# Window attention and a two-layer network in float32: weight-sum stores spread over a walk, two small tiles moved, and other start times for some DVE and ACT steps

## The chip, the cores and the metric

One Trainium2 chip, of which one core runs the kernel. The metric is the time of one execution on the device in microseconds (us); less is better.

## The reference

Sliding-window attention (8 batches, 8 heads, 576 positions, head size 64, window 64) feeds a network with a leaky activation:

```python
scores = scale * np.matmul(q, k.transpose(0, 1, 3, 2))
mask = (rel >= 0) & (rel < window)                     # rel = query position - key position, window 64
scores = np.where(mask, scores, -1000000000.0)
scores = scores - np.max(scores, axis=-1, keepdims=True)
attn = np.exp(scores)
attn = attn / (np.sum(attn, axis=-1, keepdims=True) + 1e-09)
attn_out = np.matmul(attn, v)
x = np.ascontiguousarray(attn_out.transpose(0, 2, 1, 3)).reshape(B * S, H * D)   # 4608 x 512
h = x @ w_in                                           # 512 x 2048
g = np.maximum(0.01 * h, h)
out = g @ w_out                                        # 2048 x 512
```

Everything is float32.

## The kernel before, in words

**Products.** A float32 product is made of three matmuls on a high and a low part of each operand (high x high, high x low, low x high). So every operand of the network exists twice, and a "high" step (ACT, a copy that rounds) is followed by a "low" step (DVE, what the rounding left).

**Stages.** The 4608 tokens are nine chunks of 512; the attention works on pairs of units (64 query positions of one batch each), `m` = 0 to 35. PE goes through these stages:

1. An order written out by hand (0 to about 130 us): attention of the first pairs, the first chunk, and the conversion of all weights into high and low parts (`bits`, `sign`, `abs`, `clamp`, `join`, `chi`, `rest`).
2. A walk of 32 steps `n` (about 129 to 352 us). A step has a first product (12 matmuls, line 855, in two halves), then on ACT the activation (line 869) and the high part (line 872), on DVE the low part `gs` (line 875, called low(n) below), and two steps later a second product (4 groups of 3, line 864). So the first product of step n + 2 stands on PE behind low(n).
3. For six chunks, seven products instead of eight on halves of the operands (`m`, line 1006), their sums on DVE (line 1015), the activation and the split, and the second product (`y`, line 1031), in three phases up to the end. `x_build` (lines 790 to 835) makes the sums of the attention's results that these products need.

The attention of pairs 8 to 35 is woven into stages 2 and 3. For one pair: S scores (PE, line 266); E scale and mask (DVE, 650); P the largest over partitions (POOL, 659); B subtract (DVE, 666); X exp (ACT, 670); A the sum over partitions (POOL, 662); c brings the sum's row into a tile of 128 x 8 (a DMA on SP, 673; one for each half, 64 partitions each); I adds 1e-9 and inverts (DVE, 677 and 678); rows writes it to HBM (SP, 681); spread reads it back over 64 partitions (SP, 694, twice); V the product with the values (PE, 706); take (ACT, 713); Y multiplies by the inverse (DVE, 717); keep stores the pair's result (SP, 720). From pair 20 on there is no take, and Y reads PSUM. The target of c, `compact0` or `compact1`, is used by every second pair; A of the next pair overwrites the tile `late_o` that c reads, so A waits for that DMA.

**Weight sums.** The seven products need sums of weight blocks. 40 stores on SP's DMA queue (24 of 256 KB to `w_first`, 16 of 512 KB to `w_second`: 14.7 MB) write them from the tiles in which the converted weights stand (`both`, named p or pfew in the profile; line 623). They are read again by POOL's DMAs (line 993) in stage 3.

**What sets the order.** Stages 2 and 3 are ordered by a planner in the kernel (`op`, `load`, `bulk`, `arrange`): each step has an engine, an estimated length, the steps that it follows, a rank, a `lag` (how long after its last predecessor it may start in the plan) and a `land` (how long a DMA's result takes). The planner always takes the earliest possible start, and among the steps that are ready then the lowest rank. Each engine and each DMA queue then executes its list in that order; the numbers themselves wait for nothing on the chip. The stores have rank 2.0, behind nearly everything that is ready, but are ready as soon as the weights are.

**Places in memory.** Tiles of the pool `const` come first in each partition, then the working tiles. Before the change the operands of the network (p, pfew, pxa, pxb) start 64 bytes past a multiple of 128; the tiles `gs0`, `gs1`, `q`, `k` are in `const` and start on multiples of 128.

Of the kernel before, what the change touches and what calls it, by code (L numbers as in the profile page):

```python
# [13 lines left out]
F32 = mybir.dt.float32  # L14
# [3 lines left out]
ALU = mybir.AluOpType  # L18
# [6 lines left out]
P = 128  # L25
# [58 lines left out]
FT = DF // P  # L84
# [13 lines left out]
def band_attention_ffn(ctx: ExitStack, tc: tile.TileContext, qT, kB, vW, vL, w_in, w_out, eye_mask, out, outT):  # L98
    nc = tc.nc
# [18 lines left out]
    half = FT // 2  # L118
# [69 lines left out]
    def first_at(f, k, n=1):  # L188
        return w_first[:, 512 * (7 * f + k) :][:, : 512 * n]
# [205 lines left out]
    def open_room():  # L395

        e, n, f = (wk.tile([P, 512, 2], U32, tag="raw", bufs=3, name=f"late_{x}") for x in "enf")
        e, n, f = (flat(x).bitcast(F32).rearrange("p (a b) -> p a b", a=2) for x in (e, n, f))
        r = flat(wk.tile([P, NP, 2, D], F32, tag="y", bufs=1, name="late_r").rearrange("p a b c -> p a (b c)"))
        o = [wk.tile([P, 512], F32, tag="o", name=f"late_o{i}") for i in range(2)]  # L400
        later.update(e=e, n=n, f=f, r=r, o=o)

    def e_of(m):
        return probs_of if m % 3 == 0 else later["ef"[m % 3 - 1]]
# [106 lines left out]
    def load(fn, *after, rank=1.0, us=0.5, land=4.0):  # L511
        return op("SP", us, fn, *after, rank=rank, land=land)
# [72 lines left out]
        t = pairs_of_g[n % 2] if n % 4 < 2 else own(("g", n // (2 * FT)), F32R)[:, n % 2]  # L585
        return t[:, 0], t[:, 1]

    compact = [const.tile([P, 8], F32, name=f"compact{i}") for i in range(2)]
    rows = dram.tile([NU // 2, 1024], F32, name="rows")
    x_rows = dram.tile([NU // 2, P, 512], F32, name="x_rows")  # L590

# [30 lines left out]
    def store(to, f, *cut):  # L622
        nc.sync.dma_start(to, both[f][cut])

    def store_all():
        for f in range(half):
            for x, a, k in ((f, 0, 0), (f, 256, 4), (f + half, 256, 5)):
                to = first_at(f, k).rearrange("p (i c) -> p i c", i=2)
                fn = partial(store, to, x, slice(None), slice(2), slice(a, a + 256))
                stores[x].append(load(fn, *ready[x], rank=2.0))  # L630
        for f in range(FT):
            to = w_second[f // 2, :, f % 2].rearrange("p (i c) -> p i c", i=2)
            stores[f].append(load(partial(store, to, f, slice(None), slice(2, 4)), *ready[f], rank=2.0))

    store_all()

# [15 lines left out]
    def sum_of(j):  # L652
        return later["o"][j]
# [16 lines left out]
        nc.scalar.activation(e, e, AF.Exp)  # L670

    def compact_of(m, j):
        nc.sync.dma_start(compact[m % 2][64 * j : 64 * j + 64], sum_of(j)[:1].rearrange("a (p b) -> a p b", b=8))

    def inverse_of(m):
        c = compact[m % 2]
        nc.vector.tensor_scalar_add(c, c, 1e-9)
# [82 lines left out]
    def normalise(m):  # L760

        late = 0.0 if early(m) else 0.5
        o, before, two, after = at[m], at.get(m - 1, {}), at.get(m - 2, {}), at.get(min(m + 2, EARLY - 1))
        if "v" in o and before:
            o["v"]["after"].append(before["V"])
        o["I"] = op("DVE", 0.4, partial(inverse_of, m), o["c0"], o["c1"], rank=0.8 + late)
        o["rows"] = load(partial(rows_of, m), o["I"], rank=0.3 + late)
        for j in range(2):
            if m + 2 in at:
                at[m + 2][f"c{j}"]["after"].append(o["rows"])  # L770
        spread = [load(partial(spread_of, m, j), o["rows"], before.get("Y"), rank=0.3 + late) for j in range(2)]
        if early(m):
            free = [after["E1"], before.get("take"), o["I"]]
        else:
            free = [both_free if early(m - 2) else two["Y"]]
        o["V"] = op("PE", 1.0, partial(values_of, m), o.get("v"), o["X0"], o["X1"], *free, before.get("V"), rank=0.5 + late, lag=LAG if early(m) else 2 * LAG)
        kept = two.get("kept", [])
        if early(m):
            o["take"] = op("ACT", ACTS, partial(take_of, m), o["V"], *kept, rank=0.5 + late)
        o["Y"] = op("DVE", TWO if early(m) else ONE, partial(product_of, m), *spread, o.get("take"), o["V"], *kept, rank=0.8 + late)  # L780
        if m < UPC // UNITS * LEAD:
            hi = op("ACT", ACTS, partial(high_early, m), o["Y"], *x2_free, rank=0.8 + late)
            o["kept"] = [op("DVE", TWO, partial(low_early, m), hi, rank=0.8 + late)]
# [6 lines left out]
    def x_build(s, n, xt_at, xt_free, x_free):  # L790

        urge = 1.0 if s else 0.2
        m = (UPC * LEAD + 2 * UPC * s) // UNITS + 2 * n

        def raw():
            return g_tile(xt_at[0])[:, :1024].rearrange("p (i q c) -> p i q c", i=2, q=4)

        def sums():
            return g_tile(xt_at[1])[:, 1024 * (s == 0) :][:, :1024].rearrange("p (k i c) -> p k i c", k=4, i=2)

        def part(q):
            return raw()[:, :, q] if q < 4 else sums()[:, q - 4]

        def fetch(i):
            nc.sync.dma_start(g_tile(xt_at[0])[:, 512 * i : 512 * (i + 1)], x_rows[m + i])

        got = [load(partial(fetch, i), *at[m + i]["kept"], *xt_free, rank=urge) for i in range(2)]

        def sub(to, a, b):
            nc.vector.tensor_tensor(part(to), part(a), part(b), ALU.subtract)  # L810

        d = op("DVE", 0.5, partial(sub, 4, 0, 2), *got, rank=urge)
        d3 = op("DVE", 0.5, partial(sub, 6, 1, 0), *got, rank=urge)
        d2 = op("DVE", 0.5, partial(sub, 5, 1, 4), d, rank=urge)
        d4 = op("DVE", 0.5, partial(sub, 7, 3, 5), d2, rank=urge)

        def x_view(i, a, b):
            t, k = x_all(a)
            t = t.rearrange("p k i (n c) -> p k i n c", n=4)[:, k : k + b - a, i, n]
            return t.rearrange("p k (i c) -> p k i c", i=2)  # L820

        def source(a, b):
            if a < 3:
                return raw()[:, :, 1 + a : 1 + b].rearrange("p i k c -> p k i c")
            return sums()[:, a - 3 : b - 3]

        done = []
        for a, b, after in ((0, 2, got), (2, 3, got), (3, 7, [d, d2, d3, d4])):
            hi = op("ACT", 0.2 + 0.213 * (b - a), lambda a=a, b=b: nc.scalar.copy(x_view(0, a, b), source(a, b)), *after, *x_free, rank=urge)

            def low(a=a, b=b):
                nc.vector.tensor_tensor(x_view(1, a, b), source(a, b), x_view(0, a, b).bitcast(F32), ALU.subtract)
# [72 lines left out]
    for n, (c, f) in enumerate(walk):  # L905
        next_main(6 * MM, partial(early_first, n, 0), lows.get(n - 2), *ready[f], *(x2 if c == 2 else ()))
        first = next_main(6 * MM, partial(early_first, n, 1))
        if n == 0:
            next_main(12 * MM, lambda: mm2(*prev))
            s_free = None  # L910
            for i in range(4):
                s_free = op("ACT", 0.65, lambda: due.pop(0)(), main, s_free, rank=0.1)
            evicted[-1] = [s_free] * 4
            gate = op("SP", 0.02, open_room, *all_in, s_free)
        if n > 1:
            second_step(n - 2)
# [18 lines left out]
    for f in range(half):  # L935
# [22 lines left out]
        hurry = 0.4 + 0.15 * f  # L958
        freed = slot_free[14 + f % 2] if f < 2 else prepared[f - 2]
        got = [bulk(partial(fetch, i), *freed, *all_in, rank=hurry + 0.1) for i in range(2)]  # L960
        d1 = op("DVE", 0.5, partial(join_of, 2, (0, 2), (0, 3), ALU.add), *got, rank=hurry)
        d3 = op("DVE", 0.5, partial(join_of, 1, (0, 0), (0, 2), ALU.subtract), *got, rank=hurry)
        d2 = op("DVE", 0.5, partial(join_of, 0, (1, 2), (0, 0), ALU.subtract), d1, rank=hurry)
        d4 = op("DVE", 0.5, partial(join_of, 3, (0, 1), (1, 0), ALU.subtract), d2, rank=hurry)
        hi = op("ACT", 1.07, high, d1, d2, d3, d4, rank=hurry)
# [212 lines left out]
```

## Time and profile before

| what | value |
|---|---|
| time, median of 3 runs | 905.98 us (905.42 to 908.44) |
| the profiled execution's own time | 907.11 us |
| its span in the profile | 905.3 us |
| PE busy in the span | 879.0 us (97%) |
| DVE, ACT, POOL busy | 540.2, 329.5, 362.6 us |
| moved by DMA | 214.49 MB, mean 237 GB/s |

The profiled execution took 1.8 us more than its span, which lies around the first and the last instruction. PE's idle time and the time in which its granted clock is low are what a reordering can change, since the number of matmuls stays. A timeline row reads: start and length in us, engine (q: its queue, which issues DMAs), line, operation, out<-in, shape, how many; in brackets the idle time ahead of it and what ended that. In a row of the view by windows stand the length of the window, then busy time and count of PE, PE's weight loads, DVE, ACT and POOL, then the granted clock, the DMA share and GB/s.

### The profile page before, as it was taken

What the parts mean: (1) busy time and instruction counts of PE and PEld (TensorE: products, weight loads), DVE (VectorE), ACT (ScalarE), POOL (GpSimd) and SP (SyncE); (2) the same over time, 40 slices, a digit from 0 to 9 for tenths busy, and PEclk for the clock granted to TensorE, in tenths of its full rate; (3) what the DMA queues carried; (4) which work ended last, traced back from release to release, by engine and by line L of the source; (5) the groups of instructions that cost most, each with busy time, mean ns of one, the idle gap of its engine ahead of it and who ended that gap; (6) DMA issues with size and microseconds to landing.
All of it is one profiled execution on the core that took longest, in us unless ns stands there. A gap on an engine that the chain in (4) does not pass through costs nothing.

```text
span 905.3 us, 16930 instructions
## 1 busy us (share of the span) xinstructions
PE 879.0 (97%) x6874; PEld 706.9 (78%) x6874; DVE 540.2 (60%) x843; ACT 329.5 (36%) x560; POOL 362.6 (40%) x222
## 2 busy tenths in 40 slices
PE   8999999789999998999999999999999999999998
PEld 5877888578787776877887887788888888888886
DVE  7999686368566965866576756874336323332321
ACT  4666554133233353423333332332334223332221
POOL 5332003388875700877682576881000000100000
PEclk9999999989999999999999999999999999999999
DMA  9774979753567688887989787878577575555661
GB/s 326 240 253 142 340 222 369 276 165 108 162 211 241 191 299 316 259 272 240 285 266 317 258 288 252 271 245 260 193 245 273 196 240 186 185 191 188 218 222 65
DMA packets 82557, 214.49 MB, mean 237 GB/s; under 512 B 16048, under 2 KB 26416, under 8 KB 70960
## 3 DMA queue, kind: packets, MB, share of 16 engines
q0 software_dynamic: 12960, 94.38, 31.4%
q10 hardware_dynamic: 28400, 60.53, 20.4%
q1 hardware_dynamic: 41120, 58.51, 19.5%
q8 instruction: 54, 0.88, 0.4%
q14 instruction: 23, 0.19, 0.1%
HBM read 168.59 MB, written 44.68 MB: 236 GB/s over the span
## 4 chain that ended last, share of the span: by engine, by line
PE 80%; DMA 9%; DVE 7%; issue 2%; ACT 1%; POOL 1%; ACTq 0%; SPq 0%; DVEq 0%; POOLq 0%
PE y L1031 29%; PE m L1006 24%; PE h L855 6%; PE acc L864 5%; PE h L418 4%; PE acc L454 4%; PE s L266 3%; PE o L706 3%; DMA late_r<-rows 2%; DMA compact<-late_o 1%; DMA rows<-compact 1%; DMA x_rows<-late_n 1%; DVE p L946 1%; DMA raw<-w_in 1%; DVE late_n L717 1%
## 5 line engine op out<-in xcount | busy, mean ns | idle before, releaser
L1006 PE MATMUL m<-pfew,p 128*128 128x512 f32 x720 | 172.2, 393 | 5.1 <-DVE pxa L1015 5.1
L1006 PEld LDWEIGHTS m<-pfew,p 128*128 128x128 f32 x720 | 134.4, 188 | 34.5 <-DVE pxa L1015 6.0
L1031 PE MATMUL y<-gs,p 128*128 128x512 f32 x576 | 139.5, 395 | 0.0
L1031 PE MATMUL y<-pxa,p 128*128 128x512 f32 x576 | 136.5, 391 | 0.0
L1031 PEld LDWEIGHTS y<-gs,p 128*128 128x128 f32 x576 | 107.4, 187 | 26.1
L1031 PEld LDWEIGHTS y<-pxa,p 128*128 128x128 f32 x576 | 107.7, 188 | 23.4
L993 POOL DMA_DIRECT2D p<-w_second x48 | 25.7, 535 | 187.2 <-PE y L1031 142.7
L1018 ACT ACTIVATE p<-p 128x512 f32<-128x512 f32 x63 | 39.7, 631 | 114.2 <-DVE p L1015 112.2
L864 PE MATMUL acc<-p,gs 128*128 128x512 f32 x324 | 80.3, 396 | 0.0
L1006 PE MATMUL m<-pxb,p 128*128 128x512 f32 x288 | 73.3, 399 | 3.5 <-ACT p L887 2.5
L659 POOL PARTITION_ALL_REDUCE g<-late_f x20 | 36.5, 1853 | 98.8 <-DVE late_f L650 98.7
L662 POOL PARTITION_ALL_REDUCE late_o<-late_f x20 | 65.1, 3272 | 24.1 <-ACT late_f L670 14.4
L1015 DVE TENSOR_TENSOR p<-m,pxa 128x512 f32<-128x512 f32 x63 | 43.4, 689 | 50.4 <-PE m L1006 50.1
L1024 DVE TENSOR_TENSOR gs<-p,gs 128x512 fp32r<-128x512 f32 x48 | 37.1, 774 | 56.1 <-ACT gs L1021 56.1
L864 PEld LDWEIGHTS acc<-p,gs 128*128 128x128 f32 x324 | 59.9, 188 | 13.3
L993 POOL DMA_DIRECT2D p<-w_first x42 | 22.8, 543 | 114.5 <-PE m L1006 64.7
L662 POOL PARTITION_ALL_REDUCE late_o<-e x18 | 59.2, 3308 | 20.0 <-DMA compact<-late_o 14.2
L1006 PEld LDWEIGHTS m<-pxb,p 128*128 128x128 f32 x288 | 54.4, 192 | 16.0 <-ACT p L887 2.6
L1015 DVE TENSOR_TENSOR pxa<-m,pxa 128x512 f32<-128x512 f32 x57 | 39.1, 686 | 44.7 <-PE m L1006 43.4
L662 POOL PARTITION_ALL_REDUCE late_o<-late_e x18 | 59.6, 3326 | 12.3 <-ACT late_e L670 6.0
L855 PE MATMUL h<-pxa,p 128*128 128x512 f32 x228 | 57.1, 399 | 2.1 <-DVE gs L875 2.1
L1021 ACT CAST gs<-p 128x512 fp32r<-128x512 f32 x48 | 29.7, 620 | 79.4 <-PE y L1031 79.2
(139 smaller groups left out, 1336.4 us busy)
## 6 DMA issues: line engine op xcount, KB each, us to landing
p<-w_second POOLq DMA_DIRECT2D x48, 1024.0 KB, 5.1
p<-w_first POOLq DMA_DIRECT2D x42, 1024.0 KB, 5.8
v<-vL ACTq DMA_DIRECT2D x27, 512.0 KB, 5.9
raw<-w_out ACTq DMA_DIRECT2D x15, 512.0 KB, 4.2
k<-kB ACTq DMA_DIRECT2D x28, 256.0 KB, 4.0
raw<-w_in ACTq DMA_DIRECT2D x14, 512.0 KB, 3.8
late_r<-rows SPq DMA_DIRECT2D x56, 128.0 KB, 4.4
q<-qT ACTq DMA_DIRECT2D x26, 256.0 KB, 4.7
```

Of the source, the lines that this page charges most:

```text
L418: nc.tensor.matmul(ps, a[:, k, :], b[:, k, part], start=n == 0, stop=n == len(terms) - 1)
L454: nc.tensor.matmul(acc[c, i], a[:, ts], b, start=begin and n == 0, stop=end and n == 2)
L659: nc.gpsimd.partition_all_reduce(most_of(j), e_of(m)[:, j], P, ReduceOp.max)
L662: nc.gpsimd.partition_all_reduce(sum_of(j), e_of(m)[:, j], P, ReduceOp.add)
L855: nc.tensor.matmul(ps, a[:, k, :], b[:, k], start=i == 0, stop=i == len(terms) - 1)
L864: nc.tensor.matmul(acc[c, i], a[:, i * P : (i + 1) * P], b, start=begin and k == 0, stop=n in ends and k == 2)
L993: nc.gpsimd.dma_start(ring[n], of)
L1006: nc.tensor.matmul(tiles[b], w[:, 256 * i + 128 * kt : 256 * i + 128 * kt + 128], x_part(OF_X[k], j, kt), start=begin and c == 0, stop=c = ...
L1015: nc.vector.tensor_tensor(to(), tiles[b], x(), ALU.add)
L1018: nc.scalar.activation(to(), to() if b is None else tiles[b], AF.Prelu, alpha=0.01)
L1024: nc.vector.tensor_tensor(g_pair(q)[1], x(), g_pair(q)[0].bitcast(F32), ALU.subtract)
L1031: nc.tensor.matmul(tiles[i], a, b, start=f == 0 and k == 0, stop=f == FT - 1 and k == 2)
```

## The change

Three things.

1. The 40 stores are no longer planned at once. They stand in a list, in the order in which the walk's third chunk uses the weights (blocks 15, 14, 13, 12, 0, 1, ...), and `PACE` = 2 of them are planned behind the first product of each walk step from step 1 on.
2. The two tiles that c fills move from `const` to the pool of working tiles, where they take places of a tag ("sm") that the first stage used before. `const` becomes 64 bytes shorter, so all working tiles start 64 bytes lower: p, pfew, pxa and pxb now start on a multiple of 128.
3. Planner lags grow: I and Y from 0.12 to 0.3 (3.3 from pair 20 on); in `x_build` two differences and the high parts to 0.2 or 2.6; two sums of line 946 (the preparation of combined weights) to 2.0.

All instructions stay the same, in kind and number; their order changes on all five engines from the walk on.

```diff
+PACE = 2
-    compact = [const.tile([P, 8], F32, name=f"compact{i}") for i in range(2)]
+        c = [wk.tile([P, 32], F32, tag="sm", name=f"late_c{i}")[:, :8] for i in range(2)]
-    def store_all():
-        for f in range(half):
-            for x, a, k in ((f, 0, 0), (f, 256, 4), (f + half, 256, 5)):
-                to = first_at(f, k).rearrange("p (i c) -> p i c", i=2)
-                fn = partial(store, to, x, slice(None), slice(2), slice(a, a + 256))
-                stores[x].append(load(fn, *ready[x], rank=2.0))
-        for f in range(FT):
-            to = w_second[f // 2, :, f % 2].rearrange("p (i c) -> p i c", i=2)
-            stores[f].append(load(partial(store, to, f, slice(None), slice(2, 4)), *ready[f], rank=2.0))
+    stored = []
+    for f in turn_of:
+        near, far = f % half, f // half
+        for a, k in ((0, 0), (256, 4)) if far == 0 else ((256, 5),):
+            to = first_at(near, k).rearrange("p (i c) -> p i c", i=2)
+            stored.append((f, partial(store, to, f, slice(None), slice(2), slice(a, a + 256))))
+        to = w_second[f // 2, :, f % 2].rearrange("p (i c) -> p i c", i=2)
+        stored.append((f, partial(store, to, f, slice(None), slice(2, 4))))
...
+        for f, fn in stored[(n - 1) * PACE : n * PACE] if n else ():
+            stores[f].append(load(fn, first, *ready[f], rank=2.0))
...
-        o["I"] = op("DVE", 0.4, partial(inverse_of, m), o["c0"], o["c1"], rank=0.8 + late)
+        o["I"] = op("DVE", 0.4, partial(inverse_of, m), o["c0"], o["c1"], rank=0.8 + late, lag=0.3 + 6 * late)
...
-        o["Y"] = op("DVE", TWO if early(m) else ONE, partial(product_of, m), *spread, o.get("take"), o["V"], *kept, rank=0.8 + late)
+        o["Y"] = op("DVE", TWO if early(m) else ONE, partial(product_of, m), *spread, o.get("take"), o["V"], *kept, rank=0.8 + late, lag=0.3 + 6 * late)
...
-        d = op("DVE", 0.5, partial(sub, 4, 0, 2), *got, rank=urge)
-        d3 = op("DVE", 0.5, partial(sub, 6, 1, 0), *got, rank=urge)
+        d = op("DVE", 0.5, partial(sub, 4, 0, 2), *got, rank=urge, lag=3 * urge - 0.4)
+        d3 = op("DVE", 0.5, partial(sub, 6, 1, 0), *got, rank=urge, lag=3 * urge - 0.4)
...
-        d1 = op("DVE", 0.5, partial(join_of, 2, (0, 2), (0, 3), ALU.add), *got, rank=hurry)
-        d3 = op("DVE", 0.5, partial(join_of, 1, (0, 0), (0, 2), ALU.subtract), *got, rank=hurry)
+        d1 = op("DVE", 0.5, partial(join_of, 2, (0, 2), (0, 3), ALU.add), *got, rank=hurry, lag=2.0)
+        d3 = op("DVE", 0.5, partial(join_of, 1, (0, 0), (0, 2), ALU.subtract), *got, rank=hurry, lag=2.0)
```

What this does to the order, at three places. On SP's queue at the end of the weight conversion, where the first c of the walk (pair 8, line 673 before, 671 after) stands; ahead of these rows stand, before, 15 stores more. Before:

```order
58 L623 DMA w_second<-p_7_90 128x1024
59 L623 DMA w_second<-p_8_91 128x1024
60 L623 DMA w_second<-p_9_92 128x1024
61 L623 DMA w_second<-p_10_93 128x1024
62 L623 DMA w_second<-p_11_94 128x1024
63 L623 DMA w_second<-p_15_1545 128x1024
64 L623 DMA w_second<-p_16_1620 128x1024
65 L623 DMA w_first<-p_17_1768 128x2x256
66 L623 DMA w_second<-p_17_1768 128x1024
67 L673 DMA compact_1571<-late_o_1806 64x1x8
68 L673 DMA compact_1571<-late_o_1807 64x1x8
69 L673 DMA compact_1572<-late_o_1806 64x1x8
```

And of the change:

```order
41 L624 DMA w_first<-p_17_1736 128x2x256
42 L624 DMA w_second<-p_17_1736 128x1024
43 L624 DMA w_first<-p_11_94 128x2x256
44 L624 DMA w_second<-p_11_94 128x1024
45 L671 DMA late_c_1772<-late_o_1770 64x1x8
46 L624 DMA w_first<-pfew_86 128x2x256 x2
47 L671 DMA late_c_1772<-late_o_1771 64x1x8
48 L624 DMA w_second<-pfew_86 128x1024
49 L624 DMA w_first<-pfew_86 128x2x256
50 L671 DMA late_c_1773<-late_o_1770 64x1x8
51 L679 DMA rows<-late_c_1772 128x8
```

All 40 stores stood ahead of the first c; now eight do, and about two stand between every two of the attention's transfers until the walk's step 20.

On DVE near 400 us, in stage 3's first phase: the sums of the products' banks `m_3_1` to `m_3_3` (line 1015), from which the next products on PE get free banks, with Y of pair 20 (line 717 before, 715 after) and I of pair 21 (677 and 678 before, 675 and 676 after). Before:

```order
441 L717 TENSOR_TENSOR late_n<-o_3827,late_r 128x4x2x64
442 L1015 TENSOR_TENSOR pxa_36_3702<-m_3_1_4030,pxa_36_3702 128x512
443 L677 TENSOR_SCALAR compact_1572<-compact_1572 128x8
444 L678 RECIPROCAL compact_1572<-compact_1572 128x8
445 L1015 TENSOR_TENSOR pxa_36_3702<-m_3_2_4040,pxa_36_3702 128x512
```

And of the change:

```order
446 L675 TENSOR_SCALAR late_c_1773<-late_c_1773 128x8
447 L676 RECIPROCAL late_c_1773<-late_c_1773 128x8
448 L1015 TENSOR_TENSOR pxa_36_3701<-m_3_1_4032,pxa_36_3701 128x512
449 L715 TENSOR_TENSOR late_n<-o_3802,late_r 128x4x2x64
450 L1015 TENSOR_TENSOR pxa_36_3701<-m_3_2_4042,pxa_36_3701 128x512
```

I of pair 21 and the bank's first sum moved ahead of Y of pair 20. In the next group of banks, Y of pair 21 stands between `m_4_1` and `m_4_2` as before.

On DVE near 565 us, at the end of the first phase, Y of pair 29 (line 717 before, 715 after) with the last low part of `x_build` (line 832 before, 830 after), the results' copies (line 1034) and the next phase's first sums (line 1015). Before, where that low part stands 15 rows higher:

```order
585 L1034 COPY p_25_3027<-y_1_0_5067 128x512
586 L677 TENSOR_SCALAR compact_1571<-compact_1571 128x8
587 L678 RECIPROCAL compact_1571<-compact_1571 128x8
588 L1034 COPY p_23_2923<-y_1_2_5077 128x512
589 L666 TENSOR_TENSOR late_f<-late_f,g 128x512
590 L717 TENSOR_TENSOR late_n<-o_5280,late_r 128x4x2x64
591 L1015 TENSOR_TENSOR pxa_38_5562<-m_0_1_5555,pxa_38_5562 128x512
592 L1015 TENSOR_TENSOR pxa_38_5562<-m_0_2_5565,pxa_38_5562 128x512
```

And of the change:

```order
586 L675 TENSOR_SCALAR late_c_1772<-late_c_1772 128x8
587 L676 RECIPROCAL late_c_1772<-late_c_1772 128x8
588 L715 TENSOR_TENSOR late_n<-o_5362,late_r 128x4x2x64
589 L830 TENSOR_TENSOR pfew_3381<-pxa_35_3675,pfew_3381 128x4x256
590 L1034 COPY p_25_3033<-y_1_0_5084 128x512
591 L664 TENSOR_TENSOR late_f<-late_f,g 128x512
592 L1034 COPY p_23_2921<-y_1_2_5099 128x512
593 L664 TENSOR_TENSOR late_f<-late_f,g 128x512
594 L1015 TENSOR_TENSOR pxa_38_5571<-m_0_1_5564,pxa_38_5571 128x512
```

Y of pair 29 is no longer the row ahead of the next phase's first sum; it now stands ahead of the last low part of `x_build` and of both copies.

More of the change, by code (lines that the diff above doesn't have):

```diff
@@ L400, in open_room @@
         o = [wk.tile([P, 512], F32, tag="o", name=f"late_o{i}") for i in range(2)]
-        later.update(e=e, n=n, f=f, r=r, o=o)
+        c = [wk.tile([P, 32], F32, tag="sm", name=f"late_c{i}")[:, :8] for i in range(2)]
+        later.update(e=e, n=n, f=f, r=r, o=o, c=c)
     def e_of(m):
@@ L623, in store @@
         nc.sync.dma_start(to, both[f][cut])
-    def store_all():
-        for f in range(half):
-            for x, a, k in ((f, 0, 0), (f, 256, 4), (f + half, 256, 5)):
-                to = first_at(f, k).rearrange("p (i c) -> p i c", i=2)
-                fn = partial(store, to, x, slice(None), slice(2), slice(a, a + 256))
-                stores[x].append(load(fn, *ready[x], rank=2.0))
-        for f in range(FT):
-            to = w_second[f // 2, :, f % 2].rearrange("p (i c) -> p i c", i=2)
-            stores[f].append(load(partial(store, to, f, slice(None), slice(2, 4)), *ready[f], rank=2.0))
-    store_all()
+    stored = []
[6 more added lines that the diff above has]
+        stored.append((f, partial(store, to, f, slice(None), slice(2, 4))))
     def scores_of(m):
@@ L672, in compact_of @@
     def compact_of(m, j):
-        nc.sync.dma_start(compact[m % 2][64 * j : 64 * j + 64], sum_of(j)[:1].rearrange("a (p b) -> a p b", b=8))
+        nc.sync.dma_start(later["c"][m % 2][64 * j : 64 * j + 64], sum_of(j)[:1].rearrange("a (p b) -> a p b", b=8))
     def inverse_of(m):
-        c = compact[m % 2]
+        c = later["c"][m % 2]
         nc.vector.tensor_scalar_add(c, c, 1e-9)
@@ L680, in rows_of @@
     def rows_of(m):
-        nc.sync.dma_start(rows[m].rearrange("(p b) -> p b", b=8), compact[m % 2])
+        nc.sync.dma_start(rows[m].rearrange("(p b) -> p b", b=8), later["c"][m % 2])
     def done_of(m):
@@ L828, in x_build @@
         for a, b, after in ((0, 2, got), (2, 3, got), (3, 7, [d, d2, d3, d4])):
-            hi = op("ACT", 0.2 + 0.213 * (b - a), lambda a=a, b=b: nc.scalar.copy(x_view(0, a, b), source(a, b)), *after, *x_free, rank=urge)
+            hi = op("ACT", 0.2 + 0.213 * (b - a), lambda a=a, b=b: nc.scalar.copy(x_view(0, a, b), source(a, b)), *after, *x_free, rank=urge, lag=3 * urge - 0.4)
             def low(a=a, b=b):
```

## The prediction

> **What bounds the kernel now.** I read the page first, then the waits, then the windows of the stretches in which PE idles, and last the timeline around each. The page's first part:
>
> ```profile
> PE 879.0 (97%) x6874; PEld 706.9 (78%) x6874; DVE 540.2 (60%) x843; ACT 329.5 (36%) x560; POOL 362.6 (40%) x222
> ```
>
> PE is the bound: of the span of 905.3 us it leaves 905.3 - 879.0 = 26.3 us idle, some 6 of them at the two ends. A reordering can only win idle time and slow-clock time. Who makes PE wait, and what makes those wait:
>
> ```profile
> PE h L855 <- DVE gs L875: 10.0, 2, 7.9
> PE m L1006 <- DVE pxa L1015: 5.1, 3, 2.0
> POOL late_o L662 <- DMA compact<-late_o: 22.0, 6, 14.2
> DVE late_n L717 <- DMA late_r<-rows: 19.3, 7, 4.2
> ```
>
> The first two rows say that PE waits for low parts and sums on DVE; the last two that the attention's chain waits for small DMAs (c and spread). How the DMAs stand, by windows (the last three columns are granted clock, DMA share, GB/s):
>
> ```profile
> 140.00:175.00 35.00, 35.00 (x356) 28.52 (x356) 18.92 (x25) 11.41 (x21) 11.77 (x5) 1.00 1.00 374
> 175.00:190.00 15.00, 7.10 (x84) 5.13 (x83) 9.81 (x9) 3.95 (x7) 13.85 (x6) 0.77 0.31 89
> 190.00:250.00 60.00, 60.00 (x629) 48.16 (x627) 41.07 (x51) 20.55 (x37) 50.44 (x21) 1.00 0.47 142
> 250.00:313.00 63.00, 63.00 (x616) 50.34 (x612) 48.08 (x69) 20.01 (x34) 44.04 (x18) 1.00 0.72 227
> 313.00:321.00 8.00, 5.93 (x46) 4.41 (x46) 6.77 (x9) 5.49 (x10) 2.22 (x1) 0.79 0.26 80
> 353.00:361.00 8.00, 4.47 (x49) 3.38 (x39) 6.71 (x15) 3.86 (x7) 0.00 (x0) 0.79 0.57 184
> 565.00:575.00 10.00, 8.02 (x56) 6.15 (x55) 7.26 (x13) 2.99 (x6) 7.73 (x5) 0.83 0.88 280
> ```
>
> The DMA engines are full up to 175 us, then PE idles and its clock drops (0.77), and afterwards the engines are half empty. The largest stall, gap A, in the timeline:
>
> ```profile
> 147.36 1.46 DVE L239 TENSOR_TENSOR p<-w,p 128x512 fp32r<-128x512 f32 x2
> 153.70 3.23 POOL L662 PARTITION_ALL_REDUCE late_o<-late_f  x1 [0.55 <-ACT late_f L670]
> 156.83 1.86 POOL L659 PARTITION_ALL_REDUCE g<-e  x1
> 158.60 3.31 POOL L662 PARTITION_ALL_REDUCE late_o<-late_f  x1
> 156.30 9.92 SPq L623 DMA_DIRECT2D w_second<-p  x7
> 169.42 10.46 SPq L673 DMA_DIRECT2D compact<-late_o  x3
> 168.56 0.59 ACT L872 CAST gs<-h 128x512 fp32r<-128x512 f32 x1 [3.30 <-PE acc L864]
> 176.22 2.20 DVE L677 TENSOR_SCALAR compact<-compact 128x8 f32<-128x8 f32 x1 [9.14 <-DMA compact<-late_o]
> 182.65 0.68 DVE L875 TENSOR_TENSOR gs<-h,gs 128x512 fp32r<-128x512 f32 x1
> 168.54 2.89 PE L855 MATMUL h<-pxa,p 128*128 128x512 f32 x12
> 172.45 3.02 PE L864 MATMUL acc<-p,gs 128*128 128x512 f32 x12
> 183.38 2.93 PE L855 MATMUL h<-pxb,p 128*128 128x512 f32 x6 [7.90 <-DVE gs L875]
> ```
>
> POOL ends the first sum of pair 8 at 153.70 + 3.23 = 156.93 us, but its c is issued on SP only at 169.42, behind the stores. I of pair 8 waits for it on DVE until 176.22, and low(6), whose high part stood ready at 168.56 + 0.59 = 169.15, is queued behind I and a subtraction until 182.65. PE had run dry at 172.45 + 3.02 = 175.47. Had DVE been free, low(6) would have had 175.47 - 169.15 - 0.68 = 5.6 us of slack. Gap A costs 7.90 us, and behind it six matmuls take 2.93 us where twelve take 2.89, so 2.93 - 2.89/2 = 1.5 us more.
>
> The other stalls (B near 313 us, C near 354, D, E, F at 402, 415 and 567), with what DVE did ahead of B and the Y rows ahead of D, E and F:
>
> ```profile
> 308.24 6.99 POOL L662 PARTITION_ALL_REDUCE late_o<-late_e  x2 [2.60 <-ACT late_e L670]
> 308.83 2.73 DVE L717 TENSOR_TENSOR late_n<-late_n,late_r 128x512 f32<-128x512 f32 x1
> 312.19 2.32 DVE L946 TENSOR_TENSOR p<-p 128x256 f32<-128x256 f32 x1
> 315.16 3.05 PE L855 MATMUL h<-pxa,p 128*128 128x512 f32 x9 [2.07 <-DVE gs L875]
> 356.06 0.47 PE L1006 MATMUL m<-pxb,p 128*128 128x512 f32 x1 [2.51 <-ACT p L887]
> 357.54 2.50 PE L1006 MATMUL m<-pxb,p 128*128 128x512 f32 x5 [1.02 <-DVE pxb L832]
> 399.87 0.69 DVE L717 TENSOR_TENSOR late_n<-o,late_r 128x512 f32<-128x512 f32 x1 [3.80 <-DMA late_r<-rows]
> 402.26 1.66 PE L1006 MATMUL m<-pfew,p 128*128 128x512 f32 x6 [1.36 <-DVE pxa L1015]
> 413.75 0.69 DVE L717 TENSOR_TENSOR late_n<-o,late_r 128x512 f32<-128x512 f32 x1 [3.65 <-DMA late_r<-rows]
> 415.10 1.66 PE L1006 MATMUL m<-pfew,p 128*128 128x512 f32 x6 [1.71 <-DVE pxa L1015]
> 565.59 0.69 DVE L717 TENSOR_TENSOR late_n<-o,late_r 128x512 f32<-128x512 f32 x1 [4.18 <-DMA late_r<-rows]
> 567.73 1.78 PE L1006 MATMUL m<-pfew,p 128*128 128x512 f32 x6 [1.98 <-DVE pxa L1015]
> ```
>
> D, E and F have one pattern: Y stands on DVE ahead of a sum that PE needs, and waits there for its spread. B is another: two DVE operations take 2.73 and 2.32 us while POOL reduces (308.24 to 315.23).
>
> **The stores.** Eight of them now stand ahead of the first c. The last weights are converted at 147.36 + 1.46 = 148.8 us; eight stores are 4 x 256 + 4 x 512 KB = 3.1 MB, at the 374 GB/s of the window 8.4 us, and most are ready earlier. So SP should be free when pair 8's first sum ends at 156.9. From its issue to I, c took 176.22 - 169.42 = 6.8 us with the queue full, which bounds its landing: 163.7 for the first half, and for the second, after 158.60 + 3.31 = 161.9 and some 1 us of stores, 169.7. I ends by 171.9. The subtraction queued behind I needs the next sum and maximum on POOL (163.7 + 3.2 + 1.9 = 168.8), so it ends by about 173.5 and low(6) by 174.2, before 175.47 even at this bound: **gap A goes, -9.4** (7.90 + 1.5). The other end is 0, where a transfer of the chain comes 9 us later than this.
>
> The price: the remaining 11.6 MB go over about 120 us beside the walk, 97 GB/s on top of the 142 of the half-empty window, which fits under 374. On SP each c, rows and spread stands behind up to two stores. A store's issue took 9.92/7 = 1.42 us with the engines full, so a chain of three transfers is late by 0 to 8.5 us; low(n) has 5.6 us of slack as counted above. I take +1.5 for one small new stall (between 0 and rival 3 below), nearer to 0 since the engines are not full there.
>
> **The Y and I rows moved.** At D, I of pair 21 and the first sum go ahead of Y of pair 20; the second sum then follows Y directly, 400.48 instead of about 401.6 (I and a sum, 0.6 + 0.6, no longer between), so D's 1.36 shrinks by about 1.1. E: rows of pair 21 is issued earlier by the same move, up to the 3.8 us that Y of pair 20 waited, and Y of pair 21 waited 3.65; the gap of 1.71 goes wholly or by half. **-2.2** together; ends 0 and -3.1. F: Y of pair 29 moves four rows ahead of the sum that PE needs, and its I ahead of the Y before it. Gap F is 1.98 us and the window's clock of 0.83 loses 0.17 x 10 = 1.7. Of these 3.7 I take **-3.0**; ends 0 (Y as late as now, and its wait falls on the last low part of `x_build` in its place) and -3.7.
>
> The Trainium skill, "TensorE: Matmul & The Clock Gate" (Why this matters for your kernels), asks for no idle gaps of PE above about 3 us, since one window of idle halves the clock. By that rule F, a gap of 1.98 us, would cost no clock and its removal win 1.98 at most, and the sum would be 1.0 us smaller. The window around F has the clock at 0.83, so here the measurement decides.
>
> **What I cost at nothing.** B: Y and the differences of line 946 move against low(n), but POOL's long sums keep their total, so such a meeting goes or comes back elsewhere: 0, with -3.8 (2.07 and, by the window with 0.79, 0.21 x 8 = 1.7 of clock) and as much more as ends. C hangs on pair 19's transfers, whose I and Y keep their neighbours on DVE: 0, ends -5.2 (2.51 + 1.02 + 1.7) and +4.2, the length of Y's longest wait. If the attention's chain runs less far ahead than now, C is where it shows. The DVE steps with longer lags win or lose nothing themselves; what covers them is PE's queue, and without it they cost their length, 0.4 to 0.7 us.
>
> **64 bytes lower.** The one trace of a tile's place is this pair of groups, products of equal shape, with the moving operand on a multiple of 128 bytes (gs) and 64 past one (pxa):
>
> ```profile
> L1031 PE MATMUL y<-gs,p 128*128 128x512 f32 x576 | 139.5, 395 | 0.0
> L1031 PE MATMUL y<-pxa,p 128*128 128x512 f32 x576 | 136.5, 391 | 0.0
> L1006 PE MATMUL m<-pfew,p 128*128 128x512 f32 x720 | 172.2, 393 | 5.1 <-DVE pxa L1015 5.1
> L1006 PE MATMUL m<-pxb,p 128*128 128x512 f32 x288 | 73.3, 399 | 3.5 <-ACT p L887 2.5
> ```
>
> 3.0/576 = 5.2 ns a matmul lie between them. It can be the place, that one operand's place differs from the other's (then gs gains once p lies like it), or something else in gs. I take 0; ends -3.0 (gs becomes like pxa) and rival 2.
>
> The Trainium skill, "DMA: Bandwidth & Descriptors" (How a descriptor splits into AXI transactions), says that a descriptor's transactions begin at 256-byte boundaries. A row of 2 KB that starts 192 past one would be 70 beats of 32 bytes, and 68 after the move: an estimate of 3% where DMA is the limit. No run here shows it so far, and the sum leaves it out.
>
> **The sum**: -9.4 + 1.5 - 2.2 - 3.0 = -13.1 us on the profiled execution's 907.11 (span 905.3 and 1.8 around it), so 894.0; that execution is 1.1 above the median, so **892.9** beside 905.98.
>
> **Rivals.**
> 1. Only gap A goes, and the stalls of the Y pattern come back at other places, since spread's latency stays what it is: 905.98 - 9.4 + 1.5 = 898, up to 903 if more new stalls come. For it: Y waited 19.3 us in seven places, and a moved row brings no spread earlier. Against: of 28 Y rows only three stood where PE had to wait.
> 2. The other side: slower matmuls. If a moving operand on a multiple of 128 bytes is what costs 5.2 ns, the 2,772 matmuls with p, pfew, pxa or pxb moving (1,008 at line 1006 by the rows above, 576 of y, and by the program's count 768 in the walk and 420 in the first chunk) take 14.4 us more: 892.9 + 14.4 = 907.3; with only gap A gone, 912. It decides from 13.1/2,772 = 4.7 ns. For it: the difference is in groups without any wait. Against: one pair of groups, and the same operand takes part in both.
> 3. The stores make low(n) late: 8.5 us on a chain of three, less the slack, is 2.9 us, and with 1.5 of clock 4.4 for each of the pairs 8 to 13: 892.9 + 26 = 919. It decides where a store's issue takes over 5.6/6 = 0.93 us. Against: the DMA share of 0.47 and 0.72 there.
> 4. The change doesn't do what it says: the stores ahead of the first c still hold it to 169, and the time stays at 906. Against: the order and 148.8 above.
> 5. All goes well: B or C shrink too, or gs gains its 3.0: 881 to 889.
>
> **How the numbers follow.** The forecast (889 to 897, its own range) has 0.52, rival 1 0.22, rival 2 0.09, rival 3 0.04, rival 4 0.03, the good case 0.10. About 0.3%, 2.7 us, is what a measurement of this kernel can tell from no change. Faster: 0.52 + 0.22 + 0.10 = 0.84; rival 4 and half of rival 2 within: 0.07; slower: 0.09. The range of 885 to 904 leaves out rivals 2 to 4 and the lower part of the good case, together less than 0.2.
>
> **What would show it.** Right, if the profile after has no wait of PE for `gs` above 3 us near 175, c of pair 8 issued before 160, the clock at 1.00 in that window, and fewer than two gaps among D, E and F. The groups of the last fence tell the place: 391 and 395 ns as now, or moved. Wrong, if a wait for `gs` appears between 190 and 275 (rival 3), if Y still waits 4 us ahead of a sum or ahead of `x_build`'s last low part (rival 1), or if gap C grows.

## The result

| | before | after |
|---|---|---|
| median time | 905.70 us (4 runs, 902.73 to 908.44) | 882.51 us (4 runs, 879.38 to 885.29) |
| profiled execution | 907.11 us, span 905.3 | 879.38 us, span 877.6 |
| PE busy in the span | 879.0 us (97%) | 866.8 us (99%) |

The ratio after/before is 0.9744, 95% interval 0.9697 to 0.9791: 23.2 us less, by the interval between 19 and 27. The prediction said 892.9, range 885 to 904: the direction held, the gain was nearly twice the forecast, and the time lies 2.5 us below the range, in the good case of 881 to 889 that had a chance of 0.10. The profiled execution after is the fastest of its four and the one before 1.4 us above its median, so the profiles are 27.7 us apart, 4.5 more than the medians; what follows accounts for the 27.7 of this pair.

The page after says that PE lost 12.2 us of busy time though no matmul was removed, and 15.5 us of idle time (905.3 - 879.0 = 26.3 before, 877.6 - 866.8 = 10.8 now):

```profile
PE 866.8 (99%) x6874; PEld 702.3 (80%) x6874; DVE 548.5 (63%) x843; ACT 329.7 (38%) x560; POOL 364.1 (41%) x222
```

Of the waits (engine, line, what for; us in total, times, longest) these stand against the four of the prediction:

```profile
DVE late_n L715 <- DMA late_r<-rows: 4.4, 4, 2.1
POOL late_o L660 <- DMA late_c<-late_o: 1.2, 2, 0.7
PE m L1006 <- DVE p L1015: 1.2, 1, 1.2
PE h L853 <- DVE gs L873: 0.9, 1, 0.9
PE m L1006 <- DVE pxa L1015: 0.2, 1, 0.2
```

PE's wait for low(n) fell from 10.0 to 0.9 us, for the sums from 5.1 to 1.4; POOL's wait for c from 22.0 to 1.2; Y's wait for spread from 19.3 to 4.4. In the timeline after, the first c of pair 8 and what hung on it:

```profile
152.10 3.23 POOL L660 PARTITION_ALL_REDUCE late_o<-late_f  x1 [0.56 <-ACT late_f L668]
155.36 0.54 SPq L671 DMA_DIRECT2D late_c<-late_o  x1
165.35 0.37 DVE L675 TENSOR_SCALAR late_c<-late_c 128x8 f32<-128x8 f32 x1
173.65 0.59 ACT L870 CAST gs<-h 128x512 fp32r<-128x512 f32 x1 [1.00 <-PE acc L862]
174.27 0.69 DVE L873 TENSOR_TENSOR gs<-h,gs 128x512 fp32r<-128x512 f32 x1 [2.28 <-ACT gs L870]
```

c is issued 0.03 us after POOL's sum ends (152.10 + 3.23 = 155.33), I runs at 165.35 instead of 176.22, and DVE stands waiting for the high part where a low part had been waiting for DVE. All of PE's idle times from 130 us to the end:

```profile
301.66 1.67 PE L853 MATMUL h<-pxa,p 128*128 128x512 f32 x6 [0.87 <-DVE gs L873]
338.60 0.47 PE L1006 MATMUL m<-pxb,p 128*128 128x512 f32 x1 [0.29 <-issue]
339.49 1.42 PE L1006 MATMUL m<-pxb,p 128*128 128x512 f32 x5 [0.42 <-DVE pxb L830]
341.56 7.18 PE L1006 MATMUL m<-pfew,p 128*128 128x512 f32 x29 [0.41 <-DVE pfew L830]
349.90 3.00 PE L1006 MATMUL m<-pxb,p 128*128 128x512 f32 x12 [1.16 <-DVE p L1015]
535.85 1.60 PE L1006 MATMUL m<-pxb,p 128*128 128x512 f32 x6 [0.38 <-issue]
567.38 1.66 PE L1006 MATMUL m<-pfew,p 128*128 128x512 f32 x6 [0.19 <-DVE pxa L1015]
```

Of A (7.90), B (2.07), C (2.51 + 1.02), D, E (1.36, 1.71) and F (1.98), 18.55 us in all, 3.72 are left. No gap is above 1.2 us, and the granted clock is 1.00 in the windows around each: the row of 175 to 190 us, 0.77 before, is

```profile
175.00:190.00 15.00, 15.00 (x210) 12.21 (x210) 8.23 (x11) 4.46 (x8) 10.95 (x5) 1.00 0.80 257
```

The rest is in the matmuls themselves. The groups of lines 1031 and 1006 (busy us, mean ns):

```profile
L1031 PE MATMUL y<-gs,p 128*128 128x512 f32 x576 | 135.4, 390 | 0.0
L1031 PE MATMUL y<-pxa,p 128*128 128x512 f32 x576 | 136.8, 391 | 0.0
L1006 PE MATMUL m<-pfew,p 128*128 128x512 f32 x720 | 171.3, 392 | 0.6 <-DVE pfew L830 0.4 <-DVE pxa L1015 0.2
```

The products with gs moving fell from 395 to 390 ns, 4.1 us in all; those with pxa and pfew moving, which changed their place together with the weights in p, stayed within 1 us.

### The profile page after: what moved, and what is told of

Same layout as the page of the kernel before. It is cut to its first block, busy times and chain, and to the rows that moved or that the text cites. A ratio compares the mean times of both kernels' runs of the same rounds, so it can differ in the third digit from the quotient of the medians.

```text
span 877.6 us, 16928 instructions
## 1 busy us (share of the span) xinstructions
PE 866.8 (99%) x6874; PEld 702.3 (80%) x6874; DVE 548.5 (63%) x843; ACT 329.7 (38%) x560; POOL 364.1 (41%) x222
## 4 chain that ended last, share of the span: by engine, by line
PE 82%; DMA 7%; DVE 6%; issue 2%; ACT 1%; SPq 1%; ACTq 0%; POOL 0%; DVEq 0%; POOLq 0%
PE y L1031 30%; PE m L1006 25%; PE h L420 5%; PE acc L456 5%; PE h L853 5%; PE acc L862 4%; PE s L267 3%; PE o L704 2%; DMA rows<-late_c 2%; DMA late_c<-late_o 1%; DMA late_r<-rows 1%; PE o L356 1%; DMA p<-x_rows 1%; DMA raw<-w_out 1%; DMA w_second<-p 1%
## 5 line engine op out<-in xcount | busy, mean ns | idle before, releaser
L1031 PE MATMUL y<-pxa,p 128*128 128x512 f32 x576 | 136.8, 391 | 0.0
L1031 PE MATMUL y<-gs,p 128*128 128x512 f32 x576 | 135.4, 390 | 0.0
L1006 PE MATMUL m<-pxb,p 128*128 128x512 f32 x288 | 71.5, 393 | 2.2 <-DVE p L1015 1.2
L660 POOL PARTITION_ALL_REDUCE late_o<-late_e x18 | 61.6, 3442 | 11.1 <-issue 5.0
```

What stands on the lines that cost most here:

```text
L660: nc.gpsimd.partition_all_reduce(sum_of(j), e_of(m)[:, j], P, ReduceOp.add)
L1006: nc.tensor.matmul(tiles[b], w[:, 256 * i + 128 * kt : 256 * i + 128 * kt + 128], x_part(OF_X[k], j, kt), start=begin and c == 0, stop=c = ...
L1031: nc.tensor.matmul(tiles[i], a, b, start=f == 0 and k == 0, stop=f == FT - 1 and k == 2)
```

## The experiments

The change has three separable parts. With the stores alone only SP's order moves (and one DVE row); with the tiles alone no row of any engine moves; the lags move all the rest. So each part was run alone on the kernel before, then the lags were split, and some parts were taken out of the changed kernel. "Before" in each comparison is the same kernel as above, timed on the same chip beside it (905.3 to 907.2 us).

**Stores alone.** Edit: of the change's diff, `PACE`, the list `stored` and its loop in the walk.

> The kernel before with the spread stores alone (the order of the other four engines stays, only SP's order moves; tiles where they were). By the prediction's sum: gap A goes, -9.4, with +1.5 for a small new stall, so 896 to 898, and gaps B, D, E, F stay within 1 us of 2.1, 1.4, 1.7, 2.0. Rival (the stores' spread does more than gap A, since the attention's chain then runs further ahead and C or D to F shrink with it): 887 to 893.

Measured: 896.39 us beside 907.21, ratio 0.9897 (0.9859 to 0.9935), by the ratio 9.3 us less (6 to 13). Gap A is gone; the idle times of PE from 130 us on:

```profile
285.47 1.65 PE L853 MATMUL h<-pxa,pfew 128*128 128x512 f32 x6 [0.71 <-DVE gs L873]
307.02 3.06 PE L853 MATMUL h<-pxa,p 128*128 128x512 f32 x12 [2.06 <-DVE gs L873]
332.74 3.04 PE L853 MATMUL h<-pxa,p 128*128 128x512 f32 x12 [0.90 <-DVE gs L873]
347.38 0.77 PE L1006 MATMUL m<-pxb,p 128*128 128x512 f32 x1 [2.27 <-ACT p L885]
348.86 2.50 PE L1006 MATMUL m<-pxb,p 128*128 128x512 f32 x5 [0.72 <-DVE pxb L830]
395.24 2.92 PE L1006 MATMUL m<-pfew,p 128*128 128x512 f32 x6 [2.20 <-DVE pxa L1015]
560.23 1.67 PE L1006 MATMUL m<-pfew,p 128*128 128x512 f32 x6 [2.34 <-DVE pxa L1015]
```

B, C, D and F stand where they stood. Two small stalls of 0.71 and 0.90 us are new. The time is where the prediction's -9.4 and +1.5 put it, and the rival, that the stores do more, falls. Of the +1.5 only the stall of 0.71 can be put down to the stores: one like that of 0.90 stands at the same place, near 339 us, in runs with all stores at once (0.44 with the tiles alone, 0.58 with c's tiles first, 0.66 with the lags of `x_build`). E is absent here with the order of the products and sums unchanged, so single gaps of this pattern vary from kernel to kernel.

**Stores taken out of the changed kernel.** Edit: the same lines put back as before.

> The changed kernel with the stores planned at once as before; only SP's order moves. If the three parts add up: gap A of 7 to 8 us and 1.5 of clock come back, 891 to 893. If the spread stores also keep gaps C and D to F away: 894 to 898.

Measured: 890.66 us beside 905.33, ratio 0.9843 (0.9827 to 0.9858), 8 to 9 us above the changed kernel (by the medians, by the ratios). Gap A is back, and C to F are not:

```profile
183.23 2.93 PE L855 MATMUL h<-pxb,p 128*128 128x512 f32 x6 [8.24 <-DVE gs L875]
```

So A belongs to the stores, with either order of the other engines, and the rest of the gain does not depend on it.

**Four stores a step.** Edit, on the changed kernel: `PACE = 4`.

> The changed kernel with four stores for each walk step instead of two: only SP's order moves; 14 stores stand ahead of the first c instead of eight and three or four between the next ones. If gap A hung on the place of the stores ahead of c alone, it comes back in part: 14 stores are some 5 MB, 14 us at 374 GB/s, and the slack of low(6) is 5.6 us, so a gap of 0 to 4 us, 882 to 888. If any spreading is enough (c is issued before 165): no gap, 880 to 885.

Measured: 881.19 us, ratio 0.9738 (0.9721 to 0.9755), the changed kernel's time. The first c stands behind 16 stores and still goes out right behind POOL's sum:

```profile
154.40 2.62 SPq L624 DMA_DIRECT2D w_first<-pfew  x2
157.54 1.03 SPq L671 DMA_DIRECT2D late_c<-late_o  x1
```

The expectation had counted 14 stores; the rows have 16. SP is done with the sixteenth at 154.40 + 2.62 = 157.02 us, POOL's sum ends at 157.07, and c goes out 0.47 us later. So both paces tried let SP become free in time, the pace of 4 only just; what a still larger number does was not run.

**Lags alone.** Edit: all the lags of the change (I, Y, three in `x_build`, two at line 946).

> The kernel before with the longer lags alone (order on PE, DVE, ACT, POOL as after the change; stores at once as before; tiles where they were). By the prediction's sum: gaps D, E, F shrink, -5.2, gap A of 7.9 stays, so 900 to 902. Rival (gaps B and C go by the lags too, with their clock, another 9): 890 to 894. Rival (nothing, since the chain is late from gap A on): 904 to 907.

Measured: 895.18 us beside 907.21, ratio 0.9884 (0.9848 to 0.9921), 10.5 us less, twice the 5.2 that the prediction gave them. Gap A stays with 7.45 us, D, E and F are gone, B is 0.19 us, and C has become 0.63 + 0.41 + 0.41 + 1.15, and cost no clock (1.00 from 345 to 361 us). That is the rival with B and C, though 1 us slower than it said. PE's idle times in full:

```profile
184.30 2.93 PE L855 MATMUL h<-pxb,p 128*128 128x512 f32 x6 [7.45 <-DVE gs L875]
314.24 1.66 PE L855 MATMUL h<-pxa,p 128*128 128x512 f32 x6 [0.19 <-DVE gs L875]
351.72 0.47 PE L1006 MATMUL m<-pxb,p 128*128 128x512 f32 x1 [0.63 <-ACT p L887]
352.61 1.43 PE L1006 MATMUL m<-pxb,p 128*128 128x512 f32 x5 [0.41 <-DVE pxb L832]
354.68 7.19 PE L1006 MATMUL m<-pfew,p 128*128 128x512 f32 x29 [0.41 <-DVE pfew L832]
363.02 3.06 PE L1006 MATMUL m<-pxb,p 128*128 128x512 f32 x12 [1.15 <-DVE p L1015]
549.92 1.62 PE L1006 MATMUL m<-pxb,p 128*128 128x512 f32 x6 [0.23 <-issue]
```

**The lags split.** Edits, each alone on the kernel before: `lag=0.3 + 6 * late` of I and Y; the lags in `x_build`; `lag=2.0` of the two sums of line 946.

> The kernel before with the longer lags of I and Y alone. Theory a (each group of lags takes the stalls that its own steps cause): D, E and F (1.4, 1.7, 2.0 with F's clock) go, B and C stay, so 900 to 902. Theory b (I and Y stand in all the stalls but A, so their lags take them all): 895 to 897, PE's waits as with all the lags. Theory c (the lags only work together, since each reorders the whole plan): 903 to 908.

> The kernel before with the longer lags of x_build alone. Theory a: C shrinks a little, F at most a little, 903 to 906. Theory b: nothing, 905 to 908. Theory c: 903 to 908.

> The kernel before with the longer lags of the two sums of line 946 alone. Theory a: B goes (2.1 and 1.7 of clock) since the sums move away from low(25), and C shrinks, if fewer transfers of the preparation meet its chain; D, E, F stay: 899 to 903. Theory b: nothing, 905 to 908. Theory c: 903 to 908.

Measured: I and Y 897.74 us (ratio 0.9892, 0.9852 to 0.9932); `x_build` 906.90 (1.0009, 0.9986 to 1.0033); the two sums 902.48 (0.9952, 0.9929 to 0.9976), each beside 905.36. No theory has it whole: by the waits theory a is nearest (C stays with I and Y alone, and shrinks with the two sums), but I and Y took more than it said, to within 1 us of theory b. With I and Y alone, PE has no idle time at all after 356 us, and before it:

```profile
183.51 2.93 PE L855 MATMUL h<-pxb,p 128*128 128x512 f32 x6 [7.38 <-DVE gs L875]
313.78 3.06 PE L855 MATMUL h<-pxa,p 128*128 128x512 f32 x12 [0.60 <-DVE gs L875]
339.42 3.04 PE L855 MATMUL h<-pxa,p 128*128 128x512 f32 x12 [0.82 <-DVE gs L875]
354.21 0.47 PE L1006 MATMUL m<-pxb,p 128*128 128x512 f32 x1 [2.42 <-ACT p L887]
355.69 2.50 PE L1006 MATMUL m<-pxb,p 128*128 128x512 f32 x5 [1.01 <-DVE pxb L832]
```

B shrank here too, from 2.07 to 0.60, though DVE's rows ahead of it take as long as before (2.73 and 2.32 us): low(25) is later than PE by less, and the clock is 1.00 in 300 to 321 us. The lags are not needed for that. With the same two rows, 2.73 and 2.32 us, ahead of low(25), B was 2.06 us with the stores alone, 1.38 with the tiles alone and 1.89 with the lags of `x_build`, and cost no clock in any of them. With the two sums alone, Y meets POOL's sum no more. DVE and POOL ahead of low(25):

```profile
307.26 4.07 POOL L662 PARTITION_ALL_REDUCE late_o<-late_e  x1 [0.37 <-ACT late_e L670]
308.15 3.60 DVE L946 TENSOR_TENSOR p<-p 128x256 f32<-128x256 f32 x4
311.67 0.68 DVE L717 TENSOR_TENSOR late_n<-late_n,late_r 128x512 f32<-128x512 f32 x1
312.27 0.68 DVE L875 TENSOR_TENSOR gs<-h,gs 128x512 fp32r<-128x512 f32 x1
313.01 1.66 PE L855 MATMUL h<-pxa,p 128*128 128x512 f32 x6 [0.42 <-DVE gs L875]
```

Y takes 0.68 us instead of 2.73, because POOL has finished; one stretched operation (among four of line 946, 3.60 us) stands there instead of two. The clock around C is 1.00 in this run (345 to 361 us; 0.80 with I and Y alone) and its gaps are 1.51 and 0.41 us; D and E are absent too, but new gaps came at 390 us (1.92, and 1.7 of clock) and 453 (1.29), and F stayed (1.88). By the ratios the two groups give 9.8 and 4.3 us and all the lags 10.5, each some 3 us uncertain; both take most of B, so less than the sum was to be had. With I and Y's lags on top the new gaps are absent. How the two sums reach C can be read on SP. The store of pair 19 (line 720) and the fetch of it that `x_build` needs (line 805) are 7.3 us apart before (341.54 and 348.84) and 8.6 with I and Y alone, but 3.3 with the two sums alone and 5.0 with all the lags. Why the fetch follows sooner was not tested.

**Lags of `x_build` out of the changed kernel.** Edit: those three lags removed.

> The changed kernel without the longer lags of x_build. Alone they did nothing (906.9 beside 905.4), so by theory a the time stays within 2 us of the changed kernel's, 880 to 885, with no gap above 1.5 us. If they keep the other lags from causing new stalls: 885 to 890, with a gap near 575 us or near 390 us like those in the runs with one group of lags.

Measured: 881.85 us, ratio 0.9738 (0.9719 to 0.9757): the changed kernel's time, though with a gap of 1.73 us at 304 and another of 1.74 at 554, where none above 1.5 was expected; neither cost clock. In time these lags make no difference that the runs can tell.

**More lag for the early pairs.** Edit, on the changed kernel: `lag=1.3 + 4 * late` for I and Y.

> The changed kernel with lags of 1.3 for I and Y of pairs 8 to 19 (0.3 in the change) and the 3.3 of the later ones as it is. If the rest of the stalls near 301 and 340 us (0.9 and 2.3 us in sum) come from I and Y of the early pairs: 1 to 3 us less, 879 to 882. If they come from the transfers themselves: 880 to 886.

Measured: 893.30 us, ratio 0.9872 (0.9856 to 0.9889), 11 us above the changed kernel; neither expectation. One number turned C into the largest gap of any run and B into another:

```profile
321.94 1.10 DVE L808 TENSOR_TENSOR p<-p 128x256 f32<-128x256 f32 x3 [7.68 <-DMA p<-x_rows]
323.80 4.61 PE L853 MATMUL h<-pxa,p 128*128 128x512 f32 x12 [3.81 <-DVE gs L873]
336.99 0.69 DVE L715 TENSOR_TENSOR late_n<-late_n,late_r 128x512 f32<-128x512 f32 x1 [3.61 <-ACT late_n L711]
337.71 0.32 SPq L718 DMA_DIRECT2D x_rows<-late_n  x1
342.06 2.89 SPq L886 DMA_DIRECT2D out<-p  x3
347.59 0.33 SPq L803 DMA_DIRECT2D p<-x_rows  x1
353.44 0.80 PE L1006 MATMUL m<-pxb,p 128*128 128x512 f32 x1 [9.01 <-ACT pxb L827]
```

The chain behind C was placed later in the plan: Y of the last early pair waits for its copy, its store goes out at 337.71, the fetch that `x_build` needs (line 803) is issued at 347.59, behind four result stores in SP's order (the three shown and one more at 345.04), and PE waits 9.01 us. B has the same kind of cause: `x_build`'s differences for the pairs before stand on DVE ahead of low(25) and wait 7.68 us for their fetch. Later in the order is not better as such; it helps the late pairs, whose Y stands between sums that PE needs, and harms the early ones, whose Y feeds the next stage.

**Tiles alone.** Edit, on the kernel before, with no row moved on any engine:

```diff
-    compact = [const.tile([P, 8], F32, name=f"compact{i}") for i in range(2)]
+        c = [wk.tile([P, 32], F32, tag="sm", name=f"late_c{i}")[:, :8] for i in range(2)]
```

> The kernel before with c's tiles in the working pool alone, so all working tiles 64 bytes lower; the order on all engines is that of before. By the prediction's sum (place costs nothing): 905 to 906.5, y<-gs at 395 ns as before. Rival (operands of a matmul that lie alike are faster): y<-gs falls to 390 or 391 ns, the second products of the walk and the first chunk by 1 to 3 ns each, 900 to 902.

**c's tiles first.** Edit, on the kernel before: `compact` allocated ahead of `v`, so that gs and the other constant tiles move up by 64 bytes and p stays; again no row moved.

> The kernel before with c's tiles allocated as the first ones, so that gs, q, k and the other tiles in front lie 64 bytes higher, 64 past a multiple of 128 like p; p and all working tiles where they were, order of before. If it is that both operands lie alike: y<-gs at 390 or 391 ns and the same gain as in the run with the working tiles 64 bytes lower. If it is that the weights in p have to lie on a multiple of 128: y<-gs stays at 395 ns and the time at that of before. If place does nothing: the same as that.

**32 bytes more.** Edit, on the changed kernel: a tile of 32 bytes behind the last constant tile.

> The changed kernel with 32 bytes more at the end of the constant tiles: the working tiles start 32 bytes past a multiple of 128, gs stays on one; same order. If alike has to hold to 64 bytes or less: y<-gs above 390 ns, at 395 or between, and 2 to 6 us above the changed kernel (885 to 888). If only a distance of 64 bytes is slow: y<-gs at 390 ns, and the time of the changed kernel, 880 to 885.

Measured: tiles alone 904.52 us beside 907.21, ratio 0.9972 (0.9932 to 1.0013); c's tiles first 902.19, ratio 0.9949 (0.9921 to 0.9976); 32 bytes more 887.17 beside 905.36, ratio 0.9771 (0.9734 to 0.9808), 2.4 us above the changed kernel by the ratios, whose intervals overlap, and 4.7 by the medians. The times alone leave the first open: its interval takes in no change, it misses the 900 to 902 of the rival, and its profile has new stalls near 600 us (1.80 and 1.73). The groups do not leave it open. The products with gs moving, in this order:

```profile
L1031 PE MATMUL y<-gs,p 128*128 128x512 f32 x576 | 135.9, 390 | 0.0
```

```profile
L1031 PE MATMUL y<-gs,p 128*128 128x512 f32 x576 | 135.9, 390 | 0.0
```

```profile
L1032 PE MATMUL y<-gs,p 128*128 128x512 f32 x576 | 139.1, 396 | 0.0
```

390 ns whether both operands start on a multiple of 128 bytes or both 64 past one; 395 with 64 bytes between them and 396 with 32. So in these runs the place of neither operand matters by itself, only that moving operand and weights lie alike. Which mechanism does it stays open, and a distance of 128 bytes was not tried.

## Why the prediction was wrong

| term | predicted | shown |
|---|---|---|
| gap A (stores) | -9.4 | 7.90 + 1.7 of clock: -9.6; -9.3 alone, new stalls included; 8 to 9 back when taken out |
| new small stalls | +1.5 | 0.71 with the stores alone; none in the changed kernel: 0 |
| D, E, F (I and Y) | -5.2 | 5.05 + 1.7 of clock, less 0.38 + 0.19: -6.2 |
| B | 0 | 2.07 + 1.7, less 0.87: -2.9 |
| C | 0 | 3.53 + 1.7, less 0.29 + 0.42 + 0.41 + 1.16: -3.0 |
| place of the tiles | 0 | -4.1 at y<-gs |

The predicted column sums to -13.1. Three terms that the prediction put at nothing, B, C and the place, make 10.0 us of the difference; the place is the largest single one. The three parts of the change add up: by the ratios the stores alone give 9.3 us, the lags alone 10.5 and the tiles alone 2.5 (with an interval of 6.2 less to 1.2 more), 22.3 together beside the 23.2 of the change.

The right column sums to -25.8 of the 27.7 between the two profiles. About 0.7 more lies ahead of 100 us (PE is busy for 97.05 of the first 100 us instead of 96.33), and the rest is spread over groups of matmuls that each changed by about 1 us, the walk's second products among them.

**The stores.** Each step held: SP free when pair 8's sum ends, I and low(6) in time, gap A gone. No new stall with the stores alone is above 0.90 us, which agrees with the 5.6 us of slack but does not measure it. Rival 3 (low(n) late for six pairs) shows in no run, and rival 4 (c held to 169) falls with c at 155.36.

**B and C, "what I cost at nothing", is the step that failed most, 5.9 us together.** For B, the argument was that POOL's long sums keep their total, so a meeting with DVE goes or comes back elsewhere. With the two sums alone one meeting of two is left ahead of low(25) (the 3.60 us above), and PE waits 0.42 us there: what counts is not the total of the meetings but how many stand ahead of one low(n). For C the working said that pair 19's I and Y keep their neighbours on DVE. I does. Y does not: before, DVE did low(n), then Y, then four operations of line 946, and Y waited 3.16 us for its spread; after, two of those four stand ahead of Y, and it waits 0.20. And B and C were each followed by 1.7 us of lost clock, which the working named as an end and left out of the sum.

Which gap costs clock its length alone does not settle: B lost 1.7 us of clock in the profile before, and nothing with the stores alone, where it was as long (2.06). The total is steadier: the mean clock of the 19 executions of the kernel before that ran beside the stores alone was 0.987 to 0.995, in the median 0.990, and that of the changed kernel's four 0.998 to 1.000.

**D, E and F** went for the reasons given: I and Y's lags alone take them. Y of pair 29 stands no longer ahead of the needed sum. Y of pairs 20 and 21 still stands ahead of a sum, but there the first waits 0.36 us for its spread (3.80 before) and the second not at all (3.65 before). The term was too small by 1.0 us. Rival 1, whose case was that a moved row brings no spread earlier, fell with Y's own wait: 19.3 us before, 4.4 after. With a lag of 3.3 the planner puts the late Y where its spread has landed.

**The place** stood in the text with the right cause among three ("that one operand's place differs from the other's") and its price of -3.0 as an end, and was taken as 0. The same pair of rows gave rival 2 its chance. The two rows could not tell these apart; the measured -4.1 is 7 ns a matmul, not the 5.2 between the rows, since y<-gs ended below y<-pxa (135.4 against 136.8 us). The 3% that was estimated for DMA rows shows in no run: with the tiles alone the packets of the three large queues took 31.6 + 20.1 + 19.5% of a span of 901.9 us, before 31.4 + 20.4 + 19.5% of 905.3, which is 0.5% less in all.

The range failed since the forecast took the better end of one term only, where four terms came out near their better ends: they were treated as independent of each other, but B, C, D, E and F had one pattern, DVE steps that wait for a DMA or run slowly beside POOL ahead of work that PE needs, and in the changed kernel later starts made all of them smaller. That is no rule: with still later starts for the early pairs B and C grew to 3.81 and 9.01 us.

**The Trainium skill's rule on the clock**, from "TensorE: Matmul & The Clock Gate" (Why this matters for your kernels), was set against the measurement at F. The runs speak for the measurement. In the run with the stores alone above, six matmuls take 2.92 us behind a gap of 2.20, and 1.67 us behind a gap of 2.34, where the clock stays at 1.00 from 560 to 580 us. In the run with the tiles alone a gap of 1.86 us cost clock:

```profile
563.04 2.75 PE L1006 MATMUL m<-pfew,p 128*128 128x512 f32 x6 [1.86 <-DVE pxa L1015]
```

So gaps of about 2 us cost clock at some times and not at others; those up to 1.5 us in these runs did not. The Trainium skill states on the same page (What's actually happening) that the window in which the activity is watched is free-running. The trace agrees, since that lets two gaps of equal length fall differently into it.

## What to carry to other kernels

Where a planner orders the engines, a step that waits for a DMA should stand in its engine's list where its data has landed, not where it is first thought to be ready: one wrong row holds back everything behind it, and a lag in the plan moves all such rows at once. How large it may be has to be measured: 1.3 instead of 0.3 for the early pairs cost 11 us here. Bulk transfers on a queue that also carries small, urgent ones should be issued in pieces between them. When a reordering touches many rows, look for the pattern that all stalls have in common before giving each its own price, and compare groups of equal shape for a few ns between them: at 576 matmuls, 7 ns were 4 us.

## What the runs showed of the hardware

Two things I had not expected. A 128x512 float32 product took 390 ns in the mean with both operands on the same place modulo 128 bytes, on multiples as well as 64 past them, and 395 to 396 ns with 64 or 32 bytes between moving operand and weights; start to start, from the single matmuls of the last third of the trace, that is 226.7 against 233.3 ns (after and before the change). And the halved clock behind a gap of PE of about 2 us comes in some cases and not in others with no difference in the gap's length, as the rows of 2.20, 2.34 and 1.86 us show; a gap that is cut to 1.2 us therefore won up to 1.7 us more than its own length. Where it came behind B, C and F in the profile before, it cost 1.7 us each time: behind F the granted clock is 0.54 from 569 to 571 us and 0.61 from 571 to 573, which is 0.46 x 2 + 0.39 x 2 = 1.7.

Open is why single executions of the changed kernel differ by 6 us (879.38 to 885.29). Their mean clocks, 0.998 and 1.000, account for some 1.8 of it.
